# Spare products of TensorE in the first two blocks, and a weight conversion in three steps

## The chip, the cores and the metric

One core of one Trainium2 chip runs the kernel. The metric is the device time of one execution in microseconds (us), and less is better. Five engines work side by side, each through its own queue in order: TensorE (PE in the rows, its weight loads PEld), VectorE (DVE), ScalarE (ACT), GpSimd (POOL) and SyncE (SP), which issues most of the DMAs. TensorE's granted clock has two levels here, 2.4 GHz (1.00 in the rows) and 1.2 GHz (0.50).

## The reference

Three layers stand one behind the other. A linear attention with a complex decay makes x, of 3072 tokens by 384; a gated layer makes

```python
xn = x / rms * rms_g
g = xn @ w_gate                       # 384 x 1536
silu = g * (1.0 / (1.0 + np.exp(-g)))
val = xn @ w_val
return (silu * val @ w_out)           # 1536 x 384
```

and a layer with eight experts sends each token to its best one:

```python
logits = xn @ en.T / tau
expert_idx = np.argmax(logits, axis=1)
...
h = np.maximum(x[mask] @ w1[e], 0.0)
out[mask] = gate_w[mask, None] * (h @ w2[e])
```

The three weights of the gated layer come as float64. They are turned into float32 on the chip, and each is split into a high and a low half (`h` and `l`), so that three products of the halves give nearly a float32 product.

## The kernel before, in words

The 3072 tokens are 24 tiles of 128. Eleven steps, `s0` to `s10`, take a tile through the attention; the last one, `s10`, leaves it transposed and split in `xth` and `xtl`. The gated layer works on blocks of two or three tiles (`BLOCKS`, the first two blocks have two each, then come six of three and one of two). For each of the twelve feature slices f (`NF` is 12) a block makes the gate product `pg` (`moe_g`, nine products of 128x128 by 128x256 in a block of two), the value product `pv` (`moe_v`), and adds to `po` (`moe_out`). All three go through `split_mm`, lines 784 to 786. `po` has one bank of PSUM for each tile of the block, under the tags `o0`, `o1` and `o2`, one buffer each. Blocks of two tiles don't use `o2`.

While the first block runs, the weights are still being converted. There are 36 units (`units`): for f = 0 to 11 one slice each of the gate, value and out weights. `conv(n)` does for unit n, in this order: three operations of VectorE that put the float32 together in the raw tile (lines 476 to 478), ScalarE's copy to the high half (481), VectorE's subtraction for the low half (482), for an out unit the whole of `fold` (three transposes `pwT` on TensorE, ScalarE's copy `wT`, six small products `pwe`, and a copy and a subtraction of eight columns, lines 491 to 499), and last the load of unit n + 3 by SyncE (468). Raw tiles have three buffers; `wT` shares three buffers of the tag `t` with the gate's `th`.

The order of work comes from keys. `at(key, fn, ...)` puts a step into a list, which is sorted by its key; a key counts roughly in microseconds of a plan, in which block 0 begins at 0. The steps are written out in that order. A planner then lays out each engine's queue when the kernel is built: with its own durations, it gives a free engine, of the instructions that are ready in its plan, the one that stands first in the list. So a step with a late key fills a place in which nothing that stands before it is ready. On the chip the queues are then fixed.

`conv(n)` has the key -18.4 + 1.85 n. In the start, before the first block, `warm.80` puts 80 products that nothing reads (`warm_up`, line 383) behind all the steps of the start; a product of this type is two instructions in the trace, so 160 rows.

Of the kernel before, what the change touches and what calls it, by code (L numbers as in the profile page):

```python
# [11 lines left out]
F32 = mybir.dt.float32  # L12
F32R = mybir.dt.float32r
I32 = mybir.dt.int32
AF = mybir.ActivationFunctionType
# [3 lines left out]
P = 128  # L19
# [14 lines left out]
T_BUFS = 3  # L34
# [11 lines left out]
MOE_US = 17.21  # L46
TILE_US = 9.37
# [53 lines left out]
SLOT = (0.0, 0.09, -0.43, 1.91, -1.0, -1.48, -0.61, -0.2, -0.3, -0.08, 0.0)  # L101
PACE = {0: 1.021, 2: 0.994}
CONV = (-18.4, 1.85)
ROUTE = 21.0
STARTUP = """
    s1.0 s1.1 s2.0 s2.1 s3a.0 s5a.0 s3a.1 s5a.1 s3b.0 s3b.1 s5b.0 s5b.1
    s4.0 s5c.0 s4.1 s5c.1 s5d.0 s5d.1 s6.0 s6.1 s7.0 s8.0 s7.1 s9.0
# [184 lines left out]
def fused_kernel(ctx: ExitStack, tc: tile.TileContext, H, q, k, v, are, aim, wg, wv, wo, g, emb, tau, w1, w2, out):  # L292
    nc = tc.nc
    B, S, DM = q.shape
# [4 lines left out]
    NF = wg.shape[0]  # L299
    wg, wv, wo = (a.bitcast(I32) for a in (wg, wv, wo))  # L300
    NC = DM // P
# [4 lines left out]
    blocks, t0 = [], 0  # L306
# [25 lines left out]
    ident = beside[:, NC * E:]  # L332
# [24 lines left out]
    psO = ps_moe.enter_context(tc.tile_pool(name="psO", bufs=1, space=bass.MemoryType.PSUM))  # L357
# [6 lines left out]
    def bank(name):  # L364
        return psA.tile([P, 512], F32, tag="a", name=name)
# [13 lines left out]
    def warm_up(n):  # L379

        b = psG.tile([P, BLK], F32, tag="g", name="warm")
        for _ in range(n):
            nc.tensor.matmul(b[:, :P], ones, ident, start=True, stop=True)

    def route_setup():
        nc.gpsimd.iota(iE, pattern=[[1, E]], base=0, channel_multiplier=0, allow_small_or_imprecise_dtypes=True)
        nc.vector.tensor_scalar(wE, iE, -1.0, float(E), op0=ALU.mult, op1=ALU.add)
        nc.vector.tensor_scalar(iM, iE, float(E), None, op0=ALU.subtract)
        nc.gpsimd.iota(tok, pattern=[[2 * S, B // 2], [P, CPB], [S, 2]], base=0, channel_multiplier=1)
        nc.gpsimd.memset(pinit, OOB)  # L390
        nc.gpsimd.dma_start(out=perm_d.rearrange("(p t) o -> p (t o)", p=P), in_=pinit)
        nc.gpsimd.memset(seen, 0.0)
        for r in range(E):
            nc.gpsimd.memset(caps[:, r:r + 1], float(CAPS[r] if r else HEAD))
        zero = moe.tile([P, DM + 1], F32, tag="stg", name="zero", bufs=STG_BUFS)
        nc.gpsimd.memset(zero, 0.0)
        t0, n = blocks[NB - 1]
        for i in range(t0, t0 + n):
            nc.sync.dma_start(out=x2d[rows(i)], in_=zero)
# [56 lines left out]
    moe = wop.enter_context(tc.tile_pool(name="moe", bufs=1))  # L456
    gv_pool = gvp.enter_context(tc.tile_pool(name="gv", bufs=1))
    WO = [wo_pool.tile([P, NF, DM + E], F32R, name=f"wo{i}") for i in range(2)]
    WG = [gv_pool.tile([P, NF, DM], F32R, name=f"wg{i}") for i in range(2)]
    WV = [gv_pool.tile([P, NF, DM], F32R, name=f"wv{i}") for i in range(2)]  # L460
    units = [(src, dst, f) for f in range(NF) for src, dst in ((wg, WG), (wv, WV), (wo, WO))]
    raw_t = {}

    def conv_load(n):
        if n < len(units):
            src, _, f = units[n]
            raw_t[n] = moe.tile([P, DM, 2], I32, tag="stg", name="raw", bufs=STG_BUFS)
            nc.sync.dma_start(out=raw_t[n].rearrange("p x t -> p (x t)"), in_=src[f])

    def conv(n):  # L470

        _, dst, f = units[n]
        raw = raw_t.pop(n)
        lo, hi = raw[:, :, 0], raw[:, :, 1]
        t = moe.tile([P, DM], I32, tag="ct", name="ct", bufs=CT_BUFS)
        nc.vector.tensor_scalar(t, hi, 3, 0x3FFFFFF8, op0=ALU.logical_shift_left, op1=ALU.bitwise_and)
        nc.vector.scalar_tensor_tensor(out=t, in0=hi, scalar=-0x40000000, in1=t, op0=ALU.bitwise_and, op1=ALU.bitwise_or)
        nc.vector.scalar_tensor_tensor(out=hi, in0=lo, scalar=29, in1=t, op0=ALU.logical_shift_right, op1=ALU.bitwise_or)
        w = hi.bitcast(F32)
        dh, dl = (x[:, f, :DM] for x in dst)  # L480
        nc.scalar.activation(dh, w, AF.Copy)
        nc.vector.tensor_tensor(out=dl, in0=w, in1=dh.bitcast(F32), op=ALU.subtract)
        if dst is WO:
            fold(f, w)
        conv_load(n + 3)

    def fold(f, w):

        b = bank("pwT")
        for c in range(NC):  # L490
            nc.tensor.transpose(b[:, c * P:(c + 1) * P], w[:, c * P:(c + 1) * P], ident)
        wT = moe.tile([P, DM], F32, tag="t", name="wT", bufs=T_BUFS)
        nc.scalar.activation(wT, b[:, :DM], AF.Copy)
        pe = bank("pwe")[:, :E]
        for c in range(NC):
            nc.tensor.matmul(pe, wT[:, c * P:(c + 1) * P], enT[c], start=c == 0, stop=c == NC - 1)
        dh, dl = (x[:, f, DM:] for x in WO)
        nc.scalar.activation(dh, pe, AF.Copy)
        nc.vector.tensor_tensor(out=dl, in0=pe, in1=dh.bitcast(F32), op=ALU.subtract)
# [21 lines left out]
    st = {}  # L521
# [361 lines left out]
    def rows(i):  # L883
        b, c = place(i)
        return slice(b * S + c * P, b * S + (c + 1) * P)
# [283 lines left out]
    def at(key, fn, *args):  # L1169
        events.append((key, len(events), fn, args))  # L1170
# [13 lines left out]
    done = set()  # L1184
    for x, step in enumerate(STARTUP.split()):
        fn, _, i = step.partition(".")
# [6 lines left out]
    at(-49.9, more_consts)  # L1193
    at(-30.0, embed)
    at(ROUTE, route_setup)
    start = 0.0
    prev = None
    for j, (t0, nt) in enumerate(blocks):
        nxt = blocks[j + 1][1] if j + 1 < NB else 0
        dur = PACE.get(j, 1.0) * (MOE_US * nt + TILE_US * nxt)  # L1200
        step = dur / NF
        for f in range(NF):
            key = start + f * step
            at(key, moe_g, j, f)
            at(key + 0.4 * step, moe_v, j, f)
            if prev is not None:
                at(key + 0.7 * step, moe_out, *prev)
                if prev[1] == NF - 1:
                    at(key + 0.71 * step, e1, prev[0])
            prev = (j, f)  # L1210
        for tl in range(nxt):
            i = t0 + nt + tl
            cad = dur / nxt
            fin = start + (tl + 1) * cad - LEAD
            gap = cad / 3
            if i in EARLY:
                begin, gap = EARLY[i]
                fin = begin + 9 * gap
            for sg in range(1, 11):
                if (f"s{sg}", i) not in done:  # L1220
                    at(fin - (10 - sg) * gap + NUDGE.get((sg, i), 0.0) + SLOT[sg], stages[sg], i)
        if j:
            jp, n = j - 1, blocks[j - 1][1]
            for tl in range(n):
                at(start + (ROUTING[0] + tl * ROUTING[1]) * step, e4, jp, tl)
            then = start + (ROUTING[0] + n * ROUTING[1] + ROUTING[2]) * step
            at(then, e2, jp)
            counted = then
            at(then + ROUTING[3] * step, e3, jp)
            at(then + ROUTING[4] * step, e5, jp)  # L1230
            per = -(-len(units) // (NB - 3))
            for x in range(per if j > 1 else 0):
                n = (j - 2) * per + x
                at(start + (6.2 + 0.6 * x) * step, conv_load, n)
                at(start + (7.8 + 0.6 * x) * step, check_weight, n)
            for x in range(3 if j > 2 else 0):
                n = (j - 3) * 3 + x
                if n < NTILE // 2:
                    at(start + (10.2 + 0.3 * x) * step, check_re, n, True)
                    at(start + (11.0 + 0.3 * x) * step, check_re, n, False)  # L1240
        start += dur
    for n in range(len(units)):
        at(CONV[0] + CONV[1] * n, conv, n)
    j = NB - 1
    t0, nt = blocks[j]
    begin = start - MOE_US * nt
# [85 lines left out]
```

## Time and profile before

| | |
|---|---|
| median of 3 runs | 1017.75 us (1010.55 to 1018.96) |
| profiled execution, its own time | 1016.29 us |
| its span, first to last instruction | 1014.5 us |
| mean granted clock of TensorE | 0.977 |
| busy in the span: PE / PEld / DVE / ACT / POOL | 957.2 / 914.2 / 666.0 / 606.6 / 115.3 us |
| PE in 40 slices of 25.4 us, busy tenths | `6968879999999999999999999999989999999995` |
| granted clock in the same slices, tenths | `9987789999999999999999999999999999999998` |

The span is what the rows are counted in; 1.79 us of the execution's time lie around it. The two rows of tenths are read one above the other: slice 1 of 40 begins at 0, slice 3 at 51, slice 7 at 152 us.

### The profile page before, as it was taken

What the parts mean: (1) busy time and instruction counts of PE and PEld (TensorE: products, weight loads), DVE (VectorE), ACT (ScalarE), POOL (GpSimd) and SP (SyncE); (2) the same over time, 40 slices, a digit from 0 to 9 for tenths busy, and PEclk for the clock granted to TensorE, in tenths of its full rate; (3) what the DMA queues carried; (4) which work ended last, traced back from release to release, by engine and by line L of the source; (5) the groups of instructions that cost most, each with busy time, mean ns of one, the idle gap of its engine ahead of it and who ended that gap; (6) DMA issues with size and microseconds to landing.
All of it is one profiled execution on the core that took longest, in us unless ns stands there. A gap on an engine that the chain in (4) does not pass through costs nothing.

```text
span 1014.5 us, 19018 instructions
## 1 busy us (share of the span) xinstructions
PE 957.2 (94%) x7225; PEld 914.2 (90%) x7225; DVE 666.0 (66%) x1672; ACT 606.6 (60%) x1103; POOL 115.3 (11%) x174
## 2 busy tenths in 40 slices
PE   6968879999999999999999999999989999999995
PEld 5957778999999999999999999999988999999995
DVE  6887888777767867967976976654656544444420
ACT  7665757867678777767776855532434443455531
POOL 2000000100000100100010010010113211332211
PEclk9987789999999999999999999999999999999998
DMA  6353433215213412512511520300327423554200
GB/s 209 98 158 115 127 117 87 41 41 149 40 37 94 129 40 79 165 40 64 180 41 40 156 58 24 118 1 16 95 72 241 157 100 105 181 180 164 100 33 23
DMA packets 75539, 99.29 MB, mean 98 GB/s; under 512 B 27327, under 2 KB 57502, under 8 KB 75440
## 3 DMA queue, kind: packets, MB, share of 16 engines
q1 hardware_dynamic: 70272, 87.30, 28.9%
q0 software_dynamic: 5168, 10.70, 3.2%
q8 instruction: 58, 0.95, 0.4%
q14 instruction: 41, 0.34, 0.1%
HBM read 88.04 MB, written 10.50 MB: 97 GB/s over the span
## 4 chain that ended last, share of the span: by engine, by line
PE 73%; issue 8%; ACT 6%; DMA 5%; DVE 4%; POOL 1%; SPq 0%; POOLq 0%; ACTq 0%; DVEq 0%
PE pg L784 5%; PE po L784 4%; PE pg L785 4%; PE pg L786 4%; PE pv L784 4%; PE po L786 4%; PE pv L786 4%; PE pv L785 4%; PE po L785 4%; PE pAT L693 3%; PE ph L784 3%; PE ph L786 3%; PE ph L785 3%; PE eo L786 2%; PE eo L784 2%
## 5 line engine op out<-in xcount | busy, mean ns | idle before, releaser
L784 PE MATMUL pg<-xth,wg 128*128 128x384 f32 (+1 forms) x324 | 108.5, 335 | 7.8 <-DVE th L799 7.4
L436 ACT ACT_TABLE_LOAD x87 | 111.6, 1283 | 1.6
L784 PE MATMUL pv<-xth,wv 128*128 128x384 f32 (+1 forms) x324 | 106.7, 329 | 2.4 <-DVE th L805 2.4
L784 PE MATMUL po<-wo,hth 128*128 128x392 f32 x288 | 101.7, 353 | 3.6 <-ACT hth L807 3.6
L786 PE MATMUL pg<-xth,wg 128*128 128x384 f32 (+1 forms) x324 | 104.6, 323 | 0.0
L785 PE MATMUL pg<-xtl,wg 128*128 128x384 f32 (+1 forms) x324 | 104.5, 323 | 0.0
L786 PE MATMUL pv<-xth,wv 128*128 128x384 f32 (+1 forms) x324 | 104.4, 322 | 0.0
L785 PE MATMUL pv<-xtl,wv 128*128 128x384 f32 (+1 forms) x324 | 104.3, 322 | 0.0
L785 PE MATMUL po<-wo,hth 128*128 128x392 f32 x288 | 99.3, 345 | 0.0
L1083 DVE SCALAR_TENSOR_TENSOR hel<-ph,heh 128x256 fp32r<-128x256 f32 (+6 forms) x72 | 39.8, 553 | 89.9 <-ACT heh L1082 86.6
L786 PE MATMUL po<-wo,htl 128*128 128x392 f32 x288 | 98.5, 344 | 0.0
L436 ACT ACTIVATE th<-pg 128x384 f32<-128x384 f32 (+1 forms) x108 | 49.1, 455 | 80.1 <-PE pg L786 76.8
L807 ACT ACTIVATE hth<-th 128x384 fp32r<-128x384 f32 (+1 forms) x108 | 52.4, 485 | 67.2 <-DVE th L805 61.9
L1051 DVE TENSOR_TENSOR wl<-raw,wh 128x768 fp32r<-128x768 f32 x64 | 59.6, 955 | 33.7 <-ACT wh L1050 26.5
L1082 ACT ACTIVATE heh<-ph 128x256 fp32r<-128x256 f32 (+6 forms) x72 | 34.9, 485 | 75.4 <-PE ph L786 74.6
L799 DVE SCALAR_TENSOR_TENSOR th<-th,pg 128x384 f32<-128x384 f32 (+1 forms) x108 | 54.6, 506 | 33.7 <-ACT th L436 30.9
L784 PE MATMUL ph<-xeh,wh 128*128 128x256 f32 (+6 forms) x216 | 75.5, 350 | 0.0
L784 PEld LDWEIGHTS pg<-xth,wg 128*128 128x128 f32 x324 | 62.1, 192 | 12.8 <-DVE th L799 9.6
L786 PE MATMUL ph<-xeh,wl 128*128 128x256 f32 (+6 forms) x216 | 73.3, 339 | 0.0
L785 PE MATMUL ph<-xel,wh 128*128 128x256 f32 (+6 forms) x216 | 73.0, 338 | 0.0
L808 DVE TENSOR_TENSOR htl<-th,hth 128x384 fp32r<-128x384 f32 (+1 forms) x108 | 55.1, 511 | 22.3 <-ACT hth L807 20.7
L1050 ACT ACTIVATE wh<-raw 128x768 fp32r<-128x768 f32 x64 | 51.2, 839 | 29.6 <-DMA raw<-in_moe_w_dram 18.5
(250 smaller groups left out, 2500.5 us busy)
## 6 DMA issues: line engine op xcount, KB each, us to landing
raw<-in_moe_w_dram SPq DMA_DIRECT2D x32, 768.0 KB
raw<-in_moe_w_gate_dram SPq DMA_DIRECT2D x24, 384.0 KB
raw<-in_moe_w_val_dram SPq DMA_DIRECT2D x24, 384.0 KB
raw<-in_moe_w_out_dram SPq DMA_DIRECT2D x24, 384.0 KB
X<-in_a_im_dram SPq DMA_DIRECT2D x24, 192.0 KB
X<-in_a_re_dram SPq DMA_DIRECT2D x24, 192.0 KB
V<-in_v_dram SPq DMA_DIRECT2D x24, 192.0 KB
x2d<-row SPq DMA_DIRECT2D x24, 192.0 KB
```

The source lines that it names most:

```text
L436: chain[0] = fn(*args, **kw)
L693: nc.tensor.matmul(b[:, h * P:(h + 1) * P], KT[:D2, h], QT[:D2, h], start=True, stop=True)
L784: nc.tensor.matmul(o, lh, rh, start=start and x == 0, stop=False)
L785: nc.tensor.matmul(o, lh, rl, start=False, stop=False)
L786: nc.tensor.matmul(o, ll, rh, start=False, stop=stop and x == n - 1)
L799: nc.vector.scalar_tensor_tensor(out=t, in0=t, scalar=1.0, in1=b, op0=ALU.add, op1=ALU.mult)
L807: nc.scalar.activation(hh, t, AF.Copy)
L808: nc.vector.tensor_tensor(out=hl, in0=t, in1=hh.bitcast(F32), op=ALU.subtract)
L1050: nc.scalar.activation(dh, rw, AF.Copy)
L1051: nc.vector.tensor_tensor(out=dl, in0=rw, in1=dh.bitcast(F32), op=ALU.subtract)
L1082: nc.scalar.activation(hh, b, AF.Relu)
L1083: nc.vector.scalar_tensor_tensor(out=hl, in0=b, scalar=0.0, in1=hh.bitcast(F32), op0=ALU.max, op1=ALU.subtract)
```

## The change

Two parts. `keep_busy(f, 8)` makes eight products, for each f, of the converted gate weights with themselves (128x128 by 128x384), into a tile under the tag `o2` that nothing reads: 96 products in all. They need the high half of gate unit f alone. They stand in the list at one key, 17.21 x 4 + 9.37 x 3 = 96.95, which lies in the second block. And `conv` ends with the copy to the high half; `split_weight` does the subtraction, the transposes and the copy `wT`, and the load of unit n + 3, at a key 1.2 units later (2.22); the rest of `fold` comes 2.3 units after `conv` (4.26).

```diff
+SPLIT = (1.2, 2.3)
+IDLE = 8
...
+    def keep_busy(f, n):
+
+        if "idle" not in st:
+            st["idle"] = psO.tile([P, 512], F32, tag="o2", name="idle")
+        w = WG[0][:, f]
+        for _ in range(n):
+            nc.tensor.matmul(st["idle"][:, :DM], w[:, :P], w[:, :DM], start=True, stop=True)
...
-        w = hi.bitcast(F32)
+        st["w", n] = hi.bitcast(F32)
+        nc.scalar.activation(dst[0][:, f, :DM], st["w", n], AF.Copy)
+
+    def split_weight(n):
+
+        _, dst, f = units[n]
+        w = st.pop(("w", n))
         dh, dl = (x[:, f, :DM] for x in dst)
-        nc.scalar.activation(dh, w, AF.Copy)
         nc.vector.tensor_tensor(out=dl, in0=w, in1=dh.bitcast(F32), op=ALU.subtract)
         if dst is WO:
-            fold(f, w)
+            b = bank("pwT")
+            for c in range(NC):
+                nc.tensor.transpose(b[:, c * P:(c + 1) * P], w[:, c * P:(c + 1) * P], ident)
+            st["wT", f] = moe.tile([P, DM], F32, tag="t", name="wT", bufs=T_BUFS)
+            nc.scalar.activation(st["wT", f], b[:, :DM], AF.Copy)
         conv_load(n + 3)
 
-    def fold(f, w):
-
-        b = bank("pwT")
-        for c in range(NC):
-            nc.tensor.transpose(b[:, c * P:(c + 1) * P], w[:, c * P:(c + 1) * P], ident)
-        wT = moe.tile([P, DM], F32, tag="t", name="wT", bufs=T_BUFS)
-        nc.scalar.activation(wT, b[:, :DM], AF.Copy)
+    def fold(f):
+
+        wT = st.pop(("wT", f))
         pe = bank("pwe")[:, :E]
...
+    for f in range(NF):
+        at(MOE_US * (blocks[0][1] + blocks[1][1]) + TILE_US * (blocks[1][1] + 1), keep_busy, f, IDLE)
     for n in range(len(units)):
         at(CONV[0] + CONV[1] * n, conv, n)
+        at(CONV[0] + CONV[1] * (n + SPLIT[0]), split_weight, n)
+        if n % 3 == 2:
+            at(CONV[0] + CONV[1] * (n + SPLIT[1]), fold, n // 3)
```

## Rows read from the trace of the kernel before

**Rows 1.** Busy time by stretch: start:end and length in us, then each engine.

```profile
0.00:50.00 50.00, 40.30 (x396) 35.95 (x397) 39.04 (x108) 32.97 (x58) 6.73 (x33) 1.00 0.49 152
50.00:172.00 122.00, 97.46 (x766) 88.50 (x765) 98.64 (x243) 77.16 (x150) 3.36 (x10) 0.86 0.41 120
172.00:1014.50 842.50, 819.43 (x6067) 789.74 (x6065) 528.28 (x1322) 496.46 (x896) 105.24 (x131) 0.99 0.31 91
```

**Rows 2.** The same view, the stretches at half clock; the sum is of six.

```profile
core 0: us, PE busy (x) PEld busy (x) DVE busy (x) ACT busy (x) POOL busy (x), PEclk, DMA share, GB/s
60.07:63.48 3.41, 3.41 (x18) 3.41 (x17) 3.30 (x10) 1.31 (x3) 0.00 (x0) 0.50 0.51 171
...
141.99:148.82 6.83, 6.51 (x31) 6.44 (x32) 5.70 (x14) 4.38 (x10) 0.76 (x1) 0.50 0.36 114
sum 34.14, PE 32.60 PEld 31.65 DVE 27.28 ACT 20.64 POOL 1.52; mean PE 5.43 PEld 5.28 DVE 4.55 ACT 3.44 POOL 0.25
```

**Rows 3.** The chain that ended last, in order of time: start, length, what.

```profile
22.00 0.87 PE ptQT L676 x8
...
76.00 1.77 PE ptQT L676 x8
...
118.51 0.33 PE po L784
118.84 0.33 PE po L785
```

**Rows 4.** All engines in order of time, around 150 us: start, length, instruction.

```profile
150.28 0.34 PE L784 MATMUL po<-wo,hth 128*128 128x392 f32 x1
150.46 0.34 PE L785 MATMUL po<-wo,hth 128*128 128x392 f32 x1
```

**Rows 5.** TensorE's waits, 50 to 170 us: total, times, longest.

```profile
PE pwe L496 <- ACT wT L493: 6.2, 8, 2.0
PE pwT L491 <- issue: 5.8, 3, 2.7
PE pg L784 <- DVE th L799: 4.9, 4, 2.7
PE po L784 <- ACT hth L807: 3.6, 1, 3.6
```

**Rows 6.** VectorE's waits, same stretch and columns.

```profile
DVE wo L499 <- ACT wo L498: 6.2, 8, 1.7
DVE wg L482 <- ACT wg L481: 2.6, 2, 1.4
DVE wv L482 <- ACT wv L481: 2.3, 1, 2.3
```

**Rows 7.** The view of rows 4 around one out unit, 138 to 143 us.

```profile
138.88 0.35 DVE L476 TENSOR_SCALAR ct<-raw 128x384 int32<-128x384 int32 x1
...
140.47 0.56 DVE L478 SCALAR_TENSOR_TENSOR raw<-raw,ct 128x384 int32<-128x384 int32 x1
...
141.13 0.60 PE L491 MATMUL pwT<-beside,raw 128*128 128x128 f32 x3 [2.66 <-issue]
...
142.31 0.38 PE L496 MATMUL pwe<-beside,wT 128*128 128x8 f32 x1 [0.58 <-ACT wT L493]
```

**Rows 8.** TensorE in order of time, 39 to 48 us: start, length, instructions.

```profile
39.17 0.52 PE L773 MATMUL pxT<-beside,XN 128*128 128x128 f32 x3
39.53 5.30 PE L383 MATMUL warm<-beside,ones 128*128 128x128 f32 x46
44.73 0.55 PE L773 MATMUL pxT<-beside,XN 128*128 128x128 f32 x3
```

**Rows 9.** SyncE's queue in order of time: the load of rows 7's unit.

```profile
129.33 0.35 SPq L468 DMA_DIRECT2D raw<-in_moe_w_out_dram  x1
```

**Rows 10.** Line 476, all 36: what VectorE waited for before it (us, times).

```profile
  DMA raw<-in_moe_w_val_dram: 0.2, 1
```

**Rows 11.** The end of the first block: rows leave `po`, first and last start.

```profile
L828 ACT ACTIVATE row<-po x2: 473/478/483, 172.1 to 172.5; 128x384 f32<-128x384 f32 x2
```

## Prediction

> **What bounds the kernel now.** Look first at the busy time by stretch [rows 1]. After 172 us TensorE is busy for 819.4 of 842.5 us: there the time is TensorE's own work, and what begins later ends later. The room lies ahead of that. From 50 to 172 us, which is most of the first block and the rest of the conversion, TensorE is busy for 97.5 and VectorE for 98.6 of 122 us: neither is full, and the granted clock is 0.86. So this stretch is bounded by two engines that wait for each other in turn.
>
> Second, the half-clock stretches [rows 2]. There are six, 34.1 us together, all between 60 and 149 us, and TensorE is busy for 32.6 us of them. What it does there takes twice as long: eight transpose rows take 0.87 us at full clock and 1.77 us at half, and the products of `po` start every 0.33 us at half clock and every 0.18 us at full [rows 3, 4]. Work of 32.6 us at half clock is 16.3 us at full. So the true work of TensorE in the stretch is 97.5 - 16.3 = 81.2 us, and 122 - 97.5 = 24.5 us are idle.
>
> Third, who waits for whom. Of TensorE's idle time, 6.2 us (8 times) are waits of `pwe` for the copy `wT`, 5.8 us waits of the transposes `pwT` for the converted raw tile, 4.9 and 3.6 us waits of the gated layer [rows 5]. VectorE waits 6.2 us for the eight columns of `fold` and 2.6 + 2.3 us for the copy to the high half [rows 6]: 11.1 us of its 122 - 98.6 = 23.4 us of idle time come from the conversion's inner chain. One out unit shows it [rows 7]: VectorE ends line 478 at 141.03, the transposes start at 141.13 after TensorE has stood still for 2.66 us ("issue" there, but the times say that it was line 478), and `pwe` starts after 0.58 us more of standing still, behind `wT`. All later work of TensorE stands in its queue behind these two.
>
> **The clock term.** The spare products shall fill the idle time so that the clock doesn't fall. The start shows that it can be so: there 46 warm-up rows lie in one wait between two groups of `pxT` [rows 8], and up to 50 us the clock is 1.00 [rows 1]. The bounds of what comes back are 0 and 16.3 us. How much is a question of supply. There are twelve bunches of 8, one for each gate unit, and each may start only when its unit has its high half; with late keys they are taken up greedily, in the first gaps of the plan. A bunch lasts 8 x 0.18 = 1.44 us [rows 4]. Per gate unit there are 24.5 / 12 = 2.0 us of idle time now, and (24.5 + 16.3) / 12 = 3.4 us once all runs at full clock. So the bunches cover between 42% and 72% of the idle time, and some half-clock stretches stay. I take 9 of the 16.3 us, three or four of the six stretches.
>
> The Trainium skill (TensorE: Matmul & The Clock Gate, part 1) speaks against so large a term: it says that for modelling the ramp costs under 1% of a typical kernel's span. By that rule no more than an estimated 10.1 us could come back. The six stretches add up to 16.3 us, 1.6% of the span, so this trace disagrees.
>
> **The conversion in three steps.** No instruction is added or taken away; the subtraction, the transposes with `wT`, and the rest of `fold` get later keys. In between, each engine takes work that was behind them. What can go on TensorE is the 6.2 us before `pwe`, on VectorE the 11.1 us, and these overlap in time, since both are the same chain seen from two queues. Bounds: 11.1 us of gain, and below nothing, a loss if a conversion that ends later holds up the slices that need it: the nearest row for that is the gate's wait for `th`, 4.9 us now, and I allow as much again. I take 4 us of gain, about two thirds of the `pwe` waits. The waits of `pwT` for line 478 stay, since `conv` itself keeps its key.
>
> What moves with it: the load of unit n + 3 is now issued at the second step, up to 1.2 units later in SyncE's queue. The out unit of [rows 7] begins at 138.88, and its load was issued at 129.33 [rows 9], 9.6 us earlier; line 476 waited for a load once in 36 times, 0.2 us [rows 10]. A load runs three units ahead, so a unit takes about 9.6 / 3 = 3.2 us there, and a delay of 1.2 units, 3.8 us, stays under the cover: nothing. Were the cover gone, each unit would add what its load is late. GpSimd's queue isn't passed by anything. `wT` keeps one of the three buffers of `t` longer; two are left for `th`, of which one or two live at a time: nothing. The spare tile sits in `o2`, which the first two blocks don't use; the third one, which does, begins a whole block after the last conversion: nothing.
>
> **The spare products' own price.** 96 x 0.18 = 17.3 us at full clock, 96 x 0.33 = 31.7 us at half [rows 3, 4]. One that lies in a wait costs nothing; one that stands before a product that is ready delays it and all behind it, and a bunch whose gate unit is late holds up everything queued behind on TensorE until ScalarE has copied that unit (the gate products behind it would wait for the same unit, steps of the attention would not; the nearest rows for such a wait are 0.6 to 2.7 us [rows 5, 7]). Bounds: 0, and 17.3 us if none lies in a true wait. The waits of the plan are not those of the chip, as the 2.66 us of [rows 7] shows: in the plan other work would have been put there. By totals 17.3 us go into at least 24.5 us of idle time. I put 70% of them into true waits and 30% in the way: 5 us lost.
>
> **The sum.** 9 + 4 - 5 = 8 us of gain in the stretch, 122 to 114 us. What is late next: VectorE has 98.6 us of work there, and with the waits that aren't the conversion's (23.4 - 11.1 = 12.3 us) 110.9 us. So VectorE stops the gain at about 11 us unless its other waits shrink too; 8 lies inside. TensorE would then have 81.2 + 17.3 us of work at full clock, plus some of the half-clock loss, in 114 us. Behind the stretch TensorE is busy for 97% of the time, so the 8 us pass to the end. From the profiled execution's 1016.29 us this gives 1008.3; the median of the runs is 1.46 us above it and would make 1009.8. I give 1008, just under 1.0% less than the median. A difference of about 1% is what a measurement of this kernel can tell from no change, so the forecast lies at that edge.
>
> **The rivals.**
> *The clock comes back whole and VectorE follows.* The waits of VectorE for TensorE and ScalarE shrink when TensorE is quicker. For it: up to 50 us the clock holds, with spare rows alone. Against it: 1.44 us in a bunch against 3.4 us to fill. Sum: 16.3 + 4 - 5 = 15 us: 1001.
> *The wait is VectorE's.* TensorE is made quicker where it would wait anyway, the clock still falls in most stretches (3 us come back), the three steps give 2, the spare products cost 5: 1016. For it: VectorE is 81% busy in the stretch, and at 142 us TensorE stood for VectorE's line 478 [rows 7]. Against it: TensorE is on the chain for most of the stretch, at half clock too [rows 3].
> *The spare products stand in the way.* The queue is in order, so one mechanism can turn it round: the plan's gaps lie where the chip has none. The gain of 9 + 4 = 13 us is used up from 13 / 0.18 = 72 of the 96 products on; with all 96 in the way and the clock giving 3, it is 17.3 - 3 = 14 us lost: 1030. Against it: the warm-up rows, placed by the same planner, lie in true waits [rows 8], and the idle time is larger than the supply. The Trainium skill (TensorE: Matmul & The Clock Gate, part 2) says that products keep program order and only weight loads are pulled ahead, so nothing in the chip would put that right; no row here shows a product overtaking.
> *It doesn't do what it says.* The planner leaves the bunches at their key, in the second block, where TensorE is full: 17.3 us lost, 4 won by the three steps: 1029.6. Against it: the warm-up rows again, whose key stands behind all steps of the start, and which lie between them.
>
> **How the numbers follow.** The forecast 0.50, with its own range 1003 to 1014; clock whole 0.17; VectorE's wait 0.20; in the way 0.08; not what it says 0.05. Faster by over 1% (under 1007.6): the clock's 0.17 and not quite half of the forecast, 0.40. Slower by over 1% (over 1027.9): most of the last two, 0.10. Within: 0.50. The range: its low end is the rival with the whole clock and 2 us for the spare products, 999; its high end takes in VectorE's wait and a loss of 4 us, 1020; outside stay the two slow cases and a little on the other side.
>
> **What would show it.** The granted clock from 50 to 172 us, above all how many half-clock stretches are left of six (I say two or three). The 96 products in the trace: how many follow a wait or end in one. `pwe`'s waits for `wT` under 2.5 us instead of 6.2, VectorE's for the conversion under 6 instead of 11.1. The rows of the first block leaving `po` at about 164 instead of 172.1 us [rows 11]. The forecast is wrong if the clock holds and that time doesn't move (VectorE), or if the spare products show after 172 us.

## Result and profile after

The changed kernel takes 999.33 us (median of 4 runs, 995.92 to 1003.18) against 1016.23 us for the kernel before (four runs now): ratio 0.9851, 95% interval [0.9803, 0.9898]. That is 15 us (10 to 20) less; 8 were forecast. The profiled execution of after took 1001.35 us, its span is 999.6 us, 14.9 less than before's. Executions of one kernel spread: 59 of the kernel before, taken beside the experiments, lie between 1007.52 and 1020.74 us, at mean granted clocks from 0.988 down to 0.969, and a profile shows one execution.

All lines of the kernel behind `keep_busy` have moved: the split products are 799 to 801 now, `pwT` 501, `wT` 503, `pwe` 511, the eight columns 513 and 514, the conversion 486 to 490 and the subtraction 497. First the end of the first block, the same row as [rows 11]:

```profile
L843 ACT ACTIVATE row<-po x2: 491/492/492, 155.1 to 155.6; 128x384 f32<-128x384 f32 x2
```

The rows leave `po` at 155.1 instead of 172.1 us. So 17.0 us are won up to there, and 17.0 - 14.9 = 2.1 us are lost behind it. Then the busy time by stretch, as in [rows 1], cut at that end, and two of the stretches at half clock:

```profile
0.00:50.00 50.00, 40.25 (x398) 35.69 (x399) 38.78 (x108) 33.03 (x59) 6.38 (x33) 1.00 0.49 153
50.00:155.10 105.10, 97.92 (x852) 89.20 (x851) 96.20 (x242) 75.69 (x150) 3.36 (x10) 0.98 0.46 140
...
107.02:110.43 3.41, 3.41 (x10) 2.20 (x10) 1.93 (x6) 1.35 (x3) 0.00 (x0) 0.52 0.45 150
...
755.43:758.85 3.42, 3.42 (x16) 3.42 (x15) 2.37 (x4) 1.15 (x3) 2.51 (x4) 0.50 0.97 334
```

The start is as it was. The middle stretch has 105.1 us instead of 122, with the same work of VectorE but for 2.4 us (96.2 against 98.6), so VectorE's idle time went from 23.4 to 8.9 us, and TensorE's from 24.5 to 7.2. The clock is 0.98 in place of 0.86, and of the six half-clock stretches [rows 2] one of 3.4 us is left, the line at 107 us. The waits, to be read against [rows 5] and [rows 6]: engine, what it waited for, us in total, times, longest.

```profile
PE pwe L511 <- ACT wT L503: 1.0, 2, 0.6
PE pg L799 <- DVE th L814: 1.0, 1, 1.0
PE pwT L501 <- issue: 0.8, 1, 0.8
```

```profile
DVE wo L514 <- ACT wo L513: 1.9, 2, 1.7
DVE wg L497 <- ACT wg L490: 1.2, 2, 1.0
...
DVE wo L497 <- ACT wo L490: 0.2, 1, 0.2
```

`pwe` waits 1.0 us instead of 6.2, `pwT` 0.8 instead of 5.8, `pg` 1.0 instead of 4.9; VectorE waits 3.3 us for the conversion's inner chain (1.9 + 1.2 + 0.2) where it waited 11.1. Last, where the spare products lie, TensorE in order of time, two rows of before and then after:

```profile
53.42 0.60 PE L491 MATMUL pwT<-beside,raw 128*128 128x128 f32 x3 [0.99 <-PE pv L786]
...
59.49 0.39 PE L784 MATMUL pg<-xth,wg 128*128 128x256 f32 x1 [2.66 <-DVE th L799]
```

```profile
52.02 2.08 PE L393 MATMUL idle<-wg 128*128 128x384 f32 x11
53.94 0.51 PE L501 MATMUL pwT<-beside,raw 128*128 128x128 f32 x3
...
56.16 3.02 PE L393 MATMUL idle<-wg 128*128 128x384 f32 x16
59.02 0.28 PE L799 MATMUL pg<-xth,wg 128*128 128x256 f32 x1
...
194.30 0.34 PE L629 MATMUL L<-Xl,triR 128*128 128x384 f32 x1
194.47 2.07 PE L393 MATMUL idle<-wg 128*128 128x384 f32 x11
196.38 0.28 PE L799 MATMUL pv<-xth,wv 128*128 128x256 f32 x1
```

At 52 and 56 us two groups stand where TensorE stood still before, ahead of `pwT` and of `pg`. 85 of the 96 lie before the end of the first block; the last 11 run at 194 us, in the second block, where TensorE stood for nothing: from 194.47 to 196.38 they hold it for 1.9 us. They aren't the whole loss behind the first block. Near 750 us after has two stretches at half clock of 3.4 us each, at 738 and at 755 us (the second is the line above), where before has one, at 756 us; the one more is worth an estimated 1.7 us, half of its busy time. TensorE's idle time behind the block is 1.9 us shorter than before's (844.5 - 823.3 against 842.4 - 819.3), which hides part of both.

### The profile page after: what moved, and what is told of

Its sections match the earlier page's. It is cut to its first block, busy times and chain, and to the rows that moved or that the text cites. A ratio compares the mean times of both kernels' runs of the same rounds, so it can differ in the third digit from the quotient of the medians.

```text
span 999.6 us, 19213 instructions
## 1 busy us (share of the span) xinstructions
PE 961.5 (96%) x7321; PEld 917.9 (92%) x7321; DVE 663.9 (66%) x1672; ACT 605.2 (61%) x1103; POOL 116.5 (12%) x174
## 4 chain that ended last, share of the span: by engine, by line
PE 70%; issue 8%; DVE 8%; ACT 6%; DMA 6%; POOL 1%; SPq 0%; POOLq 0%; ACTq 0%; DVEq 0%
PE pg L799 4%; PE po L799 4%; PE po L801 4%; PE pg L800 4%; PE pv L800 4%; PE pv L799 4%; PE pg L801 4%; PE pv L801 4%; PE po L800 4%; PE pAT L708 3%; PE ph L799 3%; PE ph L801 3%; PE ph L800 3%; PE eo L801 2%; PE eo L800 2%
## 5 line engine op out<-in xcount | busy, mean ns | idle before, releaser
L799 PE MATMUL pg<-xth,wg 128*128 128x384 f32 (+1 forms) x324 | 107.1, 330 | 2.7 <-DVE th L814 2.3
L799 PE MATMUL pv<-xth,wv 128*128 128x384 f32 (+1 forms) x324 | 105.7, 326 | 0.2 <-DVE th L820 0.2
L801 PE MATMUL pg<-xth,wg 128*128 128x384 f32 (+1 forms) x324 | 103.6, 320 | 0.0
L801 PE MATMUL pv<-xth,wv 128*128 128x384 f32 (+1 forms) x324 | 103.1, 318 | 0.0
```

Source lines behind the costliest of these rows:

```text
L799: nc.tensor.matmul(o, lh, rh, start=start and x == 0, stop=False)
L801: nc.tensor.matmul(o, ll, rh, start=False, stop=stop and x == n - 1)
```

## Experiments

Twelve kernels. The table has for each the ratio to the kernel before with its interval, and from its one profiled execution the length from 50 us to the end of the first block, the idle time of TensorE and VectorE in it (length less busy time), the granted clock there, and the rest of the span behind it.

| kernel | ratio, 95% interval | length | TensorE idle | VectorE idle | clock | rest |
|---|---|---|---|---|---|---|
| before | 1 | 122.1 | 24.5 | 23.4 | 0.86 | 842.4 |
| after | 0.9851 [0.9803, 0.9898] | 105.1 | 7.2 | 8.9 | 0.98 | 844.5 |
| spare products alone | 0.9913 [0.9881, 0.9945] | 113.2 | 10.4 | 14.7 | 0.95 | 842.0 |
| the same, 8 columns | 1.0031 [1.0007, 1.0055] | 125.3 | 16.6 | 26.4 | 0.84 | 844.0 |
| three steps alone | 0.9833 [0.9804, 0.9861] | 108.2 | 16.8 | 12.0 | 0.91 | 840.6 |
| both, 8 columns | 0.9868 [0.9837, 0.9899] | 110.8 | 10.5 | 14.5 | 0.91 | 840.7 |
| both, bunches of 16 | 0.9892 [0.9864, 0.9921] | 108.5 | 1.3 | 11.8 | 0.98 | 846.0 |
| both, ten bunches | 0.9846 [0.9787, 0.9905] | 107.7 | 6.9 | 11.7 | 0.94 | 841.2 |
| both, bunches of 4 | 0.9912 [0.9887, 0.9937] | 103.8 | 11.6 | 7.4 | 1.00 | 846.2 |
| steps: only the rest of fold later | 0.9914 [0.9883, 0.9945] | 111.8 | 21.7 | 12.6 | 0.91 | 841.0 |
| steps: only subtraction, transposes later | 0.9907 [0.9876, 0.9938] | 112.6 | 19.9 | 15.3 | 0.89 | 841.2 |
| steps nearer | 0.9874 [0.9840, 0.9908] | 111.0 | 20.0 | 12.9 | 0.91 | 840.0 |
| steps farther | 0.9897 [0.9863, 0.9930] | 112.1 | 18.6 | 16.2 | 0.88 | 843.4 |
| before, keys nudged | 1.0001 [0.9973, 1.0029] | 126.8 | 24.0 | 27.6 | 0.81 | 842.8 |

Half-clock time follows from the clock: 2 x (1 - 0.86) x 122.1 = 34 us before.

The theory to begin with was that the clock carries most of the 15 us, with the steps for a smaller part. The rival was that the steps carry it.

**Spare products alone** (`conv` as before):

```diff
+    for f in range(NF):
+        at(MOE_US * (blocks[0][1] + blocks[1][1]) + TILE_US * (blocks[1][1] + 1), keep_busy, f, IDLE)
     for n in range(len(units)):
         at(CONV[0] + CONV[1] * n, conv, n)
```

> Spare products alone, the conversion in one piece as before. If the clock is the cause, the half-clock time between 50 and 160 us falls from 34 to under 10 us and the time is 1001 to 1007, most of the gain. If the three steps are the cause, half-clock time may fall, but the time stays at 1012 to 1018.

1006.71 us, 0.9913: 9 us of gain. The stretch in it:

```profile
50.00:163.20 113.20, 102.83 (x863) 95.16 (x862) 98.50 (x243) 76.57 (x151) 3.37 (x10) 0.95 0.44 130
```

Half-clock time falls from 34 to 10 us (two stretches, 10.2 us). The clock theory's number, at its upper end; but the next run takes away its first place.

**Three steps alone** (after, with no spare product):

```diff
-IDLE = 8
+IDLE = 0
```

> The three steps alone, no spare product. Clock theory: half-clock time stays above 20 us, TensorE's waits for wT shrink from 6.2 to about 1 us, and the time is 1010 to 1014 (2 to 6 us of gain). Steps theory: 999 to 1004, as with both.

999.53 us, 0.9833: 17 us of gain, as much as both parts together. The steps theory's number, and the clock theory's sum falls. Its stretch, and its waits on TensorE and VectorE:

```profile
50.00:158.20 108.20, 91.41 (x772) 82.67 (x771) 96.25 (x243) 76.19 (x151) 3.37 (x10) 0.91 0.46 137
```

```profile
PE pg L799 <- DVE th L814: 4.1, 3, 2.2
...
PE pwT L501 <- DVE raw L488: 2.2, 2, 1.4
...
PE pwe L511 <- ACT wT L503: 1.2, 2, 0.6
...
DVE wg L497 <- ACT wg L490: 4.6, 4, 3.2
DVE wo L514 <- ACT wo L513: 1.9, 2, 1.7
```

The waits for `wT` and for the eight columns are as short as with both parts; the other waits of TensorE are longer, and so is VectorE's for the gate's high half (4.6 us against 1.2). And the clock rises without any spare product, to 0.91: 20 us at half clock instead of 34. Those three stretches, and the two of the spare products alone, in the view of [rows 2]:

```profile
sum 20.48, PE 19.56 PEld 18.86 DVE 16.12 ACT 11.17 POOL 0.00; mean PE 6.52 PEld 6.29 DVE 5.37 ACT 3.72 POOL 0.00
```

```profile
sum 10.23, PE 10.23 PEld 9.98 DVE 8.59 ACT 7.17 POOL 0.00; mean PE 5.12 PEld 4.99 DVE 4.29 ACT 3.58 POOL 0.00
```

Half of TensorE's busy time at half clock is what the half clock costs, an estimate as in the prediction: 16.3 us before, 9.8 with the steps alone, 5.1 with the spare products alone. Busy time less that cost is 81.3 us before and 81.6 with the steps alone: the work is the same. So of the 13.9 us by which the steps alone shorten the stretch, some 6.5 are clock and 7.7 are idle time (24.5 to 16.8 us).

**Both, with 8 columns in place of 384**, a control with nearly the same queues and less work. In the traces the rows of TensorE, VectorE and ScalarE stand in the order of the three steps alone, with the 96 added; after's order differs in 115 of TensorE's other 7225 rows and 35 of VectorE's 1672.

```diff
-            nc.tensor.matmul(st["idle"][:, :DM], w[:, :P], w[:, :DM], start=True, stop=True)
+            nc.tensor.matmul(st["idle"][:, :8], w[:, :P], w[:, :8], start=True, stop=True)
```

> Both parts, but each spare product has 8 columns in place of 384: the same 96 places in nearly the same queues, hardly any work in them. Clock theory: the half-clock stretches come back (over 20 us) and the time is that of the three steps alone, 1010 to 1014. If the order in the queues is the cause: 997 to 1002, since the products' own price is gone as well.

1002.76 us, 0.9868. The half-clock time is back at 2 x 0.09 x 110.8 = 20 us as the clock theory said, but the time is nearer to the rival's: some 16 us less half-clock time shorten the stretch by 110.8 - 105.1 = 5.7 us, and the whole by 0.0017 of it, 1.7 us, which two overlapping intervals don't separate from nothing. The control isn't free of work: a product of 8 columns holds TensorE for 0.11 us (the row is shown further down), one of 384 columns for 0.17.

**Both, bunches of 16**:

```diff
-IDLE = 8
+IDLE = 16
```

> Both parts, 16 products in each bunch, 192 in all, 17.3 us more work of TensorE at full clock. If the waits take them, 998 to 1002; if the waits are full with the first 96, they stand in the way: 1008 to 1017. I expect about 1008: 11 of the 96 lie already at 194 to 196 us, where TensorE has no waits.

1005.41 us, 0.9892, between the two expectations. The waits are full: TensorE idles for 1.3 us of 108.5, and 43 of the 192 products stand behind the first block (the rest is 846.0 us).

Since the clock was not the answer with the steps there, the next four ask which of the steps it is, and whether fewer products do better.

**Steps: only the rest of `fold` later**, no spare product:

```diff
-SPLIT = (1.2, 2.3)
+SPLIT = (0.0, 2.3)
```

> No spare product; of the two later keys only that of the rest of fold (2.3 units), the subtraction and the transposes directly behind conv. If the whole gain of the steps alone (999.5) comes from nobody standing still for wT and the eight columns behind it: 998 to 1003, VectorE's waits at those columns under 3 us. If it comes from the later subtraction and transposes: 1010 to 1017.

1005.25 us, 0.9914, between the two expectations: half the gain of the steps. VectorE's waits at the eight columns are short, but TensorE's for the converted tile are back. In order, TensorE and VectorE:

```profile
PE pwT L501 <- issue: 5.5, 2, 3.6
PE pg L799 <- DVE th L814: 4.7, 3, 2.5
...
PE pwT L501 <- DVE raw L488: 2.9, 2, 2.0
...
DVE wo L514 <- ACT wo L513: 1.7, 1, 1.7
```

**Steps: only subtraction and transposes later**:

```diff
-SPLIT = (1.2, 2.3)
+SPLIT = (1.2, 1.2)
```

> No spare product; subtraction, transposes and wT 1.2 units later, the rest of fold directly behind them. If the later rest of fold is the cause: 1010 to 1017, with the waits of pwe for wT back at about 6 us. If the later subtraction and transposes are: 998 to 1003.

1005.07 us, 0.9907, again half. `pwe` waits little for `wT` here too (1.2 us, where about 6 were named), so it is not the key of the rest of `fold` alone that takes those waits away. The waits at the eight columns come back, and TensorE's wait for the gate's `th` is twice that of both steps (4.1 us):

```profile
PE pg L799 <- DVE th L814: 8.6, 3, 4.0
...
PE pwT L501 <- DVE raw L488: 1.4, 1, 1.4
PE pwe L511 <- ACT wT L503: 1.2, 2, 0.6
...
DVE wo L514 <- ACT wo L513: 4.8, 6, 1.7
```

So each step has a wait of its own: the later transposes that of TensorE for line 488 (5.5 + 2.9 = 8.4 us against 1.4, if the "issue" of `pwT` is that line, as in [rows 7]), the later columns that of VectorE (4.8 against 1.7). The two gains, 0.9% each, add up to the 1.7% of both.

**Both, ten bunches**:

```diff
-    for f in range(NF):
+    for f in range(NF - 2):
```

> Both parts with bunches for f = 0 to 9 alone, 80 products. With both parts 11 of 96 lie at 194 to 196 us where TensorE has no waits, 1.9 us. If these are what the spare products give back, this is 996 to 998 and the quickest so far; if their price lies before that too, 999 to 1001, no better than the steps alone.

998.56 us, 0.9846. All 80 products lie before 127 us and the rest is 841.2 us, 3.3 less than after's; the stretch is 2.6 longer, with 0.94 of the clock. Nothing measurable is won on after: the late products' 1.9 us come out of the rest, which also has one half-clock stretch less near 750 us, and the clock in the stretch takes it back.

**Both, bunches of 4**:

```diff
-IDLE = 8
+IDLE = 4
```

> Both parts with 4 products in each bunch, 48 in all. If the clock is worth something beyond the price of the products, some three of the half-clock stretches go and the time is 995 to 998; if clock and price cancel at any dose, 998 to 1002.

1005.14 us, 0.9912, a miss for both expectations: slower than none, and by the medians than eight too, where the intervals just touch. The first block ends earliest of all here, at 153.8 us, at full clock; but in the 40 us behind it TensorE is idle for 4.5 us, against 1.3 in after, and the clock falls again:

```profile
153.80:193.80 40.00, 35.55 (x304) 33.84 (x303) 27.40 (x88) 28.42 (x54) 4.02 (x6) 0.91 0.23 48
```

The profiled execution took less than the median (span 1000.0), so this accounts for a part of it only. The mean clock doesn't explain the rest: the ten executions have 0.984 to 0.991, the six of the steps alone 0.984 to 0.987. Why four are worse than none stays open.

The last four go back to the clock in the kernel before, to a control, and to the distance of the steps.

**Spare products alone, 8 columns**: the first experiment with the edit of the third. In the traces the rows of TensorE (but for the 96), VectorE and ScalarE stand in exactly the order of before; those of the first experiment differ from it in 34 of TensorE's rows and 4 of VectorE's.

> The conversion in one piece, spare products of 8 columns: the queues are nearly those of the spare products alone (1006.7), with hardly any work in the added places. If the clock gave that gain, the half-clock stretches are back at some 30 us and the time is 1013 to 1017. If the changed order of the other work gave it: 1004 to 1009.

1019.6 us, 1.0031, over the 1013 to 1017 that were named for the clock: all of the gain is gone, and 3 us more. Here it is the clock: nearly the same queues with 384 columns in the spare products give 0.9913. The difference is 1.2%, 12 us; 9 of them are a gain on the kernel before, and 3 are what the 8-column products themselves cost there. The stretch, and one group of them:

```profile
50.00:175.30 125.30, 108.71 (x858) 101.00 (x858) 98.87 (x243) 76.78 (x149) 3.37 (x10) 0.84 0.40 116
...
51.55 2.74 PE L392 MATMUL idle<-wg 128*128 128x8 f32 x24
```

```profile
PE pwe L505 <- ACT wT L502: 6.2, 8, 2.0
```

```profile
DVE wo L508 <- ACT wo L507: 8.6, 8, 2.5
```

These waits of the conversion are about those of before, 6.2 and 6.2 us [rows 5, 6]. (Lines 505 and 508 here are 511 and 514 of after.)

**Before, keys nudged**:

```diff
-CONV = (-18.4, 1.85)
+CONV = (-18.2, 1.85)
```

> The kernel before with all conversion keys 0.2 later, nothing else: a control for what a mere reshuffle of the queues does. If a reshuffle is worth little: 1012 to 1018, within 0.4% of before. If gains of 9 us come from any reshuffle: some time well outside that, on either side.

1015.95 us, 1.0001 [0.9973, 1.0029], though 39 of TensorE's rows and 55 of VectorE's stand elsewhere in the order. This one reshuffle is worth nothing (the table's row for it is of its longest execution, 1021.41 us). It is as large as that of the spare products alone; the steps alone move 764 and 285 rows, and no reshuffle of that size without their purpose was tried.

**Steps nearer, steps farther**, no spare product:

```diff
-SPLIT = (1.2, 2.3)
+SPLIT = (1.0, 2.0)
```

```diff
-SPLIT = (1.2, 2.3)
+SPLIT = (2.2, 3.6)
```

> No spare product, the later keys at 1.0 and 2.0 units in place of 1.2 and 2.3. If the distance itself is the cause, a little less of it does nearly the same: 998 to 1004. If only this very order is good: over 1006.

> No spare product, the later keys at 2.2 and 3.6 units. The chain within the conversion has still more room, but a raw tile is held a unit longer, so loads come later and VectorE may wait for them. If there is more to win: 993 to 998; if the room was enough: 998 to 1003; if loads get late: over 1003, with waits of line 486 for raw tiles over 3 us.

1003.09 us, 0.9874, and 1006.24 us, 0.9897. So the gain is no accident of one order, and of the three distances tried 1.2 and 2.3 is the best by the medians; against the nearer one the intervals overlap. Too far isn't a matter of loads (line 486 waits 1.2 us for them, under the 3 that were named); VectorE now waits for the gated layer's copy instead:

```profile
DVE htl L823 <- ACT hth L822: 5.0, 3, 1.9
...
DVE ct L486 <- DMA raw<-in_moe_w_gate_dram: 1.2, 2, 1.0
```

No version beats after and the three steps alone beyond the intervals; these two and the ten bunches lie within each other's. The spare products can be left out.

## Why the prediction came out as it did

The time lies in the stated range (999 to 1020), 0.3 us above its low end, and the direction is right. It is below the forecast's own range (1003 to 1014), and a change under 1% had the largest chance. In size it is the case of the whole clock (1001 was its time), which had 0.17, but not in cause; that the range holds it is luck. Of the signs that were named, `pwe`'s waits (1.0 us) and VectorE's for the conversion (3.3 us) came as said; one half-clock stretch is left where two or three were expected, and the rows leave `po` at 155.1 us, not at about 164.

*The place* was right: all of the gain lies between 50 us and the end of the first block, and the rest passes it to the end but for 2.1 us.

*The steps' term* is the one that failed by size: 4 us forecast, 17 measured alone (13.9 of them in the stretch). It was taken as two thirds of `pwe`'s waits on TensorE. The step said that the waits of `pwT` for line 478 stay, since `conv` keeps its key; they went from 5.8 us to 2.7 with the steps alone (2.2 + 0.5) and 1.1 in after, because the transposes now come to TensorE's queue when the tile is ready. Without that later key they are 8.4 us. And the term left out that fewer waits leave the clock higher: 34 to 20 us of half-clock time with no spare product at all, some 6.5 us of the 13.9.

*The clock's term*, 9 us, and *the price*, 5 us, make 4 together. In the kernel before, the spare products gained 9 us: an estimated 11.2 from the clock (16.3 - 5.1), less what their 96 x 0.174 = 16.7 us of work took beyond the 14.1 us by which the idle time fell. On top of the steps both terms were sized nearly right in the stretch: 9.8 - 1.7 = 8.1 us from the clock, and 85 x 0.174 = 14.8 us of work for 9.6 us less idle time, a price of 5.2. That makes 3 us, as the stretch shows (108.2 to 105.1). Behind it after takes 3.9 us more than the steps alone (844.5 against 840.6), in which lie the late products and the one more half-clock stretch; so nothing is left, as the times say (0.9851 against 0.9833). The two parts are not additive, which the sum supposed: 9 and 17 us alone, 15 to 17 together. Both take away the same idle time of TensorE.

*The price's mechanism* was right. 85 of the 96 went to the stretch that has waits (70% were forecast to lie in one), and the sign that speaks against the forecast, spare products behind 172 us, came for the 11 others. Which of the 85 delayed something was not looked up one by one. That more of them find no wait is shown by the bunches of 16.

*VectorE as the next limit* was right in kind and too strict in number. Its work in the stretch is 96 to 99 us in every kernel, and at 105.1 us it is 92% busy. The bound of 110.9 kept 12.3 us of its other waits; these shrank too, to 8.9 us of idle time in all. "Unless its other waits shrink too" was the exception that came.

*The rivals.* That the products stand in the way as a whole happened at the double dose only; "not what it says" happened for 11 of the 96. *Nothing* was right for `t`'s buffers and the spare tile as far as the waits show. For the loads it was nearly right: VectorE waits 1.0 us for raw tiles in after (0.7 and 0.3 us) where it waited 0.2.

The Trainium skill (TensorE: Matmul & The Clock Gate, part 1) says that for modelling the ramp costs under 1% of a typical kernel's span. The prediction made of it a bound of an estimated 10.1 us for six falls in the middle of the kernel; the page says it of the ramp. As such a bound it didn't hold here: the spare products alone gave back an estimated 11.2 us of clock, 1.1% of the span.

## What to carry to other kernels

Where two engines wait for each other in turn, look for a step whose inner chain (convert, copy, transpose, copy, multiply) goes through three engines under one key, and give each link its own later place: that won 17 us here with no instruction more. Products that nobody reads buy back the clock where idle time can't be removed (9 us in the kernel before, their price paid), but here, once the waits were gone, they bought next to nothing, and those that find no wait are paid in full. Measure the two parts of a change alone before adding their gains.

## What was not expected of the hardware

TensorE's busy share and its granted clock didn't go together. From 50 us to the end of the first block it was busy for 97.6 of 122.1 us (80%) before, at a granted clock of 0.86; with 96 products of 8 columns for 108.7 of 125.3 us (87%), at 0.84; with 96 products of 384 columns for 102.8 of 113.2 us (91%), at 0.95.

A product of 8 columns is far from 48 times shorter than one of 384: 24 in a row took 2.74 us, 0.11 us each (the spare products alone, 8 columns), and 11 of 384 columns took 1.9 us, 0.17 us each (after, at 194 us).
